# A linear-attention layer and a gated expert layer in one kernel: from units chunk by chunk to units batch by batch, with some whole-batch loads

## The chip, the cores and the metric

The kernel runs on one core of a Trainium2 chip. The metric is the device time of one execution in microseconds. Three runs before the change gave 155.5, 156.43 and 154.58 us, a median of 155.5. The profile is of one execution more, with a span of 152.4 us from the first to the last instruction that it shows.

## What is computed

There are 4 batches, 8 heads, 768 tokens and 48 numbers a head. The first half is a recurrent attention with a decay for each number, the second a layer with a softmax-like gate and a normalisation:

```python
for t in range(S):                       # state: [B, H, 48, 48]
    y[t] = r[t] @ (state + (u * k[t])^T v[t])
    state = w[t][:, None] * state + k[t]^T v[t]
x = y as [B * S, H * D]                  # 3072 x 384
h = x @ w_in                             # 3072 x 1024
solu = h * softmax(h)
ln = (solu - mean(solu)) / sqrt(var(solu) + 1e-6) * g_ln
out = ln @ w_out                         # 3072 x 384
```

All inputs and the output are fp32; the matrix products are made in bf16.

## The kernel before, in words

**Units.** The 768 tokens of a batch are cut into 6 chunks of 128. A unit is one chunk of one batch, with all 8 heads: 24 units. Before, unit i is chunk i // 4 of batch i % 4 (line 117, `units`), so that the four batches take turns and a batch's state goes from unit i to unit i + 4.

**Stages.** Each unit goes through some forty stages, each a small function. The string `ORDER` (lines 21 to 67) lists every stage of every unit as a word: name, unit, and after a point where it is done (`a` ScalarE, `d` VectorE, `p` GpSimd, or a number, the bank of PSUM). The loop at the end (line 550) calls the functions word by word. The class `InOrder` (line 72) makes each engine keep this order in its own queue; SyncE, which issues all DMAs, too. So an instruction that waits holds up everything that stands behind it on its engine. Nearly all instructions carry line 86, the helper's; go by the tiles.

The words that matter here:

- `LW`, `LK`, `LR`, `LV` (lines 246 to 256): load w, k, r, v of a unit, 192 KB each, 8 heads of 48 numbers (192 B) for 128 tokens. They go into rings of 7 tiles (`NIO`), whose heads lie 64 numbers apart. k and r share the tile `kr_in`.
- `LI`, `LO`: load w_in in 3 parts and w_out in 2, into tiles of their own (`win_f`, `wout_f`); `wi` casts w_in to bf16, `gw` multiplies w_out by the gain, `mn`, `mc` and `ce` take off the column means.
- `lw` log of w (ScalarE), `cum` cumulated logs (TensorE), `ex` their exponentials (ScalarE), `kp` k and r scaled with them (VectorE), `krk` and `krr` the transposes of both (TensorE), `kr` their copy from PSUM.
- `p`, `q`, `qh`, `dg`, `dv`: the bonus term with u, on GpSimd and VectorE (`qh` folds the product in half first); `vb` the cast of v.
- `M`, `m`, `sel`: the scores of the chunk, their copy and mask. `Y`, `y`: attention out, with the state of the chunk before; `Y` with `i` adds the bonus by a product with the identity, with `n` the copy `y` adds it. `S`, `et`, `st`: the new state.
- `X`, `xT`: y transposed. `H`: the product with w_in, 24 matmuls. `e` exp, `he` h times exp, `hq` its square, `ea` two halves of e added, so that the sum of e takes 4 matmuls and not 8. `Oa`, `Ob`: the product with w_out, four of eight parts each, with the sums for the norm in three more columns of the same bank.
- `sq`, `qm`, `lv` (lines 518 to 527): the norm's scale rs = exp(-0.5 ln(...)), two ScalarE operations around one of VectorE and then two on ScalarE. `o`: the output times rs. `out`: the store of 192 KB.
- `hot`: matmuls on zeros at the start. `LU`, `us`, `uc` and `LG`, `gs`, `gc` bring u and the gain in.

**Memory.** PSUM is cut by hand into 8 banks; `H`, `M` and `cum` take two each.

Of the kernel before, what the change touches and what calls it, by code (L numbers as in the profile page):

```python
# [8 lines left out]
F32 = mybir.dt.float32  # L9
# [11 lines left out]
ORDER = """  # L21
LW2 LU0 ik0 lw2 hot5.4 cum2.0 LW1 lw1 us0.7 ih0 LW3 lw3 cum3.2 LR2 uc0 ex2 LK2 p2 LV2 vb2.p kp2 hot4.4 krk2.6 krr2
LR1 LK1 cum1.4 LW0 ex1 kp1 kr2.d hot1.0 S2.7 lw0 et2 LV1 vb1.d LW4 st2 p1 q1 hot2.0 krk1.1 krr1 q2 qh2 dg2 LG0
kr1.a M2.4 ex3 hot1.0 M1.6 m1.d dv2 LR0 LK0 p0 q0 cum0.0 ex0 lw4 cum4.6 ex4 kp0 krk0.1 krr0 LR3 gs0.0 gc0 dg1
m2.d Y2.i0 kr0.d LK3 p3 LR4 LV0 vb0.a dg0 dv1 kp3 Y1.i5 hot3.1 krk3.4 krr3 LK4 kp4 M0.2 m0.d krk4.1 y1.a X1.5
krr4 y2.a X2.0 dv0 xT2.d hot1.6 Y0.n7 y0.d kr3.a M3.2 hot1.0 X0.6 S1.4 p4 q3 kr4.a xT1.a xT0.a LI2 LI1 wi1.a
M4.0 m4.a et1 LI0 S0.5 et0 wi0.d m3.d LO1 wi2.p H1.6 e1 gw5.a H2.0 e2 H0.2 LO0 gw2.a q4 qh4 dg4 qh3 dg3 gw4.p
gw7.p LV3 vb3.p dv3 sel4 LW6 e0 gw6.d st1 LV4 vb4.p he1 lw6 dv4 gw1.d LW5 gw0.d gw3.d mn0.4 mc0 ce5.p ce6.p
Y3.i7 ce4.p he2 st0 he0 cum6.0 y3.a ce7.p hot1.5 X3.6 lw5 xT3.a ce3.d LK6 LR6 p6 Y4.n5 LR5 LK5 ce2.d hq0.a ex6
LW7 cum5.2 H3.6 p5 y4.d ex5 ce1.d ce0.d Oa0.5 kp6 krk6.1 krr6 S4.0 hq1.d Oa1.4 kp5 krk5.3 krr5 X4.2 Ob1 e3 he3  # L30
LV5 q6 q5 kr5.d hq2.a et4 st4 M5.6 kr6.a M6.0 xT4.d lw7 cum7.2 hq3.a sq1 m6.a m5.d dg5 vb5.d qm1 dv5 Ob0 ex7 sq0
qm0 S3.7 qh6 LR7 LK7 p7 kp7 et3 lv1 st3 lv0 H4.0 Y5.n6 y5.d LR9 LK8 o1.d e4 krk7.3 krr7 Oa2.2 he4 X5.7 q7 kr7.d
LW9 lw9 o0.a LK9 p9 LW8 lw8 S5.6 et5 cum9.4 ex9 Ob2 sq2 LR8 p8 st5 dg6 kp9 qm2 LV6 xT5.a LV9 vb6.p dv6 sel6
cum8.0 ex8 kp8 hq4.a LV7 LV11 out1 LW10 dg7 vb7.p dv7 Oa3.3 vb9.a lv2 H5.6 e5 M7.4 m7.d he5 q8 krk9.1 LK10 krr9
kr9.a S9.0 et9 Ob3 sq3 st9 q9 qm3 o2.a out0 ea5.p Y6.i5 y6.a LV8 LR10 Y7.n4 y7.d LW11 LW12 krk8.1 M9.6 lw10 lv3
X6.2 xT6.a m9.d o3.a krr8 LV10 out3 out2 kr8.d qh9 dg9 dg8 hq5.d cum10.4 ex10 kp10 S6.0 vb11.d et6 X7.2 xT7.a
st6 p10 vb8.d dv8 dv9 H6.6 e6 he6 H7.2 lw11 e7 he7 M8.4 m8.a Oa5.1 Y9.n0 Ob5 sq5 y9.d cum11.6 ex11 krk10.5 krr10
qm5 kr10.d S7.4 et7 st7 Oa4.3 hq6.d lv5 lw12 o5.a X9.2 sel8 Y8.i0 vb10.p y8.a LK11 LR11 kp11 xT9.d q10 dg10 p11
M10.4 m10.a sel10 S10.1 et10 st10 dv10 S8.0 et8 S11.7 et11 X8.6 xT8.a LK12 LW13 cum12.4 q11 ex12 lw13 st11 st8
Ob4 sq4 qm4 LW14 LR12 kp12 p12 lw14 lv4 o4.a out5 LK13 LV12 LR13 Y10.n2 dg11 y10.d H8.6 e8 krk12.1 krk11.0 krr11  # L40
krr12 kr12.d he8 kr11.a q12 qh12 cum13.4 H9.2 vb12.p S12.1 ex13 p13 q13 ea7.p dg12 kp13 dv11 LW16 LR14 LK14 e9
he9 et12 st12 M12.6 m12.a Oa6.0 X10.5 xT10.a krk13.4 krr13 kr13.a M11.6 m11.d ea8.p dv12 sel12 p14 cum14.2 ex14
q14 out4 Ob6 sq6 hq8.d M13.4 m13.d LV13 hq7.a LW15 lw15 lw16 kp14 vb13.d H10.6 dg13 qm6 LW18 lw18 Y11.n1 y11.d
Oa8.5 LK16 LR15 LR16 LK15 e10 he10 hq9.a krk14.4 Y12.i3 krr14 lv6 qh14 kr14.d p15 ea10.p dv13 LR18 LV14 vb14.p
q15 qh15 LK18 p18 Ob8 sq8 qm8 y12.a S13.2 et13 st13 o6.a lv8 X11.1 xT11.d cum16.6 ex16 X12.3 hq10.d LW19 kp16
Oa9.4 cum15.0 xT12.a Ob9 ex15 kp15 sq9 o8.a dg14 dv14 qm9 M14.2 m14.a sel14 krk16.7 Oa7.6 krr16 kr16.d lv9 o9.d
cum18.0 ex18 kp18 Ob7 LV15 S14.5 et14 st14 krk15.3 krr15 kr15.d LK19 Y13.i2 lw19 cum19.0 krk18.7 p16 q16 vb15.a
S15.4 y13.a sq7 qm7 dg15 X13.5 xT13.d ex19 LR19 kp19 lv7 o7.a q18 krr18 kr18.d H11.2 et15 st15 krk19.5 krr19
kr19.d LW17 lw17 cum17.0 e11 he11 ex17 ea11.p out8 LK17 LR17 p17 kp17 H12.6 e12 he12 hq11.a p19 H13.4 e13 Oa10.3
Y14.n2 M16.0 m16.a dg16 q19 dv15 y14.d ea12.p ea13.p M15.6 m15.d he13 Ob10 sq10 X14.2 out9 Oa11.1 LW20 qm10 lw20  # L50
cum20.6 hq12.d krk17.0 krr17 out6 out7 LV16 vb16.a dv16 xT14.a S16.2 LR20 ex20 LK20 dg18 et16 st16 lv10 o10.a
H14.4 e14 kp20 Ob11 sq11 kr17.d LK23 qm11 lv11 o11.a Oa12.2 krk20.3 krr20 kr20.a he14 sel16 Y16.n7 y16.d Y15.n6
y15.d M19.4 m19.a M18.0 m18.d Ob12 X15.7 xT15.a q17 hq13.d LV19 LW21 LV17 X16.3 xT16.a ea14.p vb19.a M17.4 m17.d
sq12 LK22 out10 qm12 dg17 qh19 vb17.p sel19 p20 hq14.a LW22 LV20 q20 qh20 dv17 M20.0 LV21 m20.d out11 LK21 H15.6
e15 he15 lw22 ea15.p H16.4 LV18 vb18.p dv18 LR21 p21 lw21 Oa14.3 Y17.n1 LR22 LV23 q21 dg19 dv19 Ob14 LR23 p23
p22 e16 he16 lv12 Oa13.0 LW23 o12.a out12 sq14 qm14 hq15.d vb20.a lv14 dg20 dv20 y17.d cum21.6 ex21 Ob13 cum22.4
sq13 ex22 LV22 vb22.p ea16.p o14.d out14 Y18.n2 y18.d Oa15.1 X18.3 qm13 kp22 lv13 xT18.d X17.2 xT17.a kp21 Ob15
sq15 qm15 S18.5 et18 st18 Y19.n4 y19.d lv15 o15.a out15 o13.a krk22.2 S17.3 et17 lw23 H18.6 e18 ea18.p hq16.d
vb21.d st17 Y20.n5 y20.d X19.4 xT19.d krr22 kr22.a H17.0 he18 hq18.d cum23.4 ex23 kp23 Oa16.3 e17 ea17.p he17
krk21.2 krr21 kr21.a H19.6 e19 krk23.5 X20.4 krr23 q22 qh21 vb23.p out13 xT20.a kr23.a he19 Oa18.2 Ob16 sq16  # L60
M21.0 q23 ea19.p qh23 dg22 dv22 m21.a sel21 qm16 lv16 M22.6 hq19.a M23.4 Ob18 sq18 dg21 H20.0 o16.a out16 m22.d
m23.d Oa19.7 Y22.n6 qm18 lv18 hq17.d Ob19 S19.5 dg23 dv23 e20 Oa17.4 y22.d X22.3 he20 et19 st19 xT22.d dv21
Y21.n6 Ob17 y21.d sq19 o18.a sq17 qm17 lv17 Y23.n1 out18 qm19 lv19 X21.0 xT21.d H22.2 o17.a e22 out17 ea20.p
y23.d H21.0 X23.5 xT23.a e21 hq20.d o19.d out19 Oa20.6 he22 hq22.d H23.4 e23 he21 hq21.d Ob20 sq20 qm20 lv20
o20.a out20 ea22.p Oa22.7 ea21.p Oa21.3 he23 hq23.d Ob22 sq22 qm22 lv22 Ob21 sq21 qm21 lv21 o21.d o22.a out22
out21 ea23.p Oa23.2 Ob23 sq23 qm23 lv23 o23.a out23
"""

NIO, NLW, NKP, NWK = 7, 10, 6, 4
# [24 lines left out]
def kernel(  # L94
# [22 lines left out]
    units = [(c, b) for c in range(NC) for b in range(B)]  # L117
# [30 lines left out]
    w_t = ring("w_in", NIO, [C, H, 64], F32)  # L148
    kr_t = ring("kr_in", NIO, [C, 2, H, 64], F32)
    v_t = ring("v_in", NIO, [C, H, 64], F32)  # L150
    win_f = consts.tile([128, KM, DF], F32)
    wout_f = consts.tile([128, KF, DM], F32)
    o_t = ring("o", NWK, [C, DM], F32)
# [28 lines left out]
    dve.memset(inv_col, 1.0 / RDF)  # L182
    ones_row = consts.tile([1, C], F32)
# [23 lines left out]
    st_t = [ring(f"st{b}_", 2, [C, H, D], BF16) for b in range(B)]  # L207
    xT_t = ring("xT", NWK, [128, KM, C], BF16)
    e_t = ring("e", NWK, [128, KF, C], BF16)
    ea_t = ring("ea", NWK, [128, KF // 2, C], BF16)  # L210
    he_t = ring("he", NWK, [128, KF, C], BF16)
    hq_t = ring("hq", NWK, [128, KF, C], BF16)
    sq_t = ring("sq", NWK, [C, 2], F32)
    qm_t = ring("qm", NWK, [C, 1], F32)
    lv_t = ring("lv", NWK, [C, 1], F32)
# [26 lines left out]
    def rows_of(src, i):  # L242
        c, b = units[i]
        return src[b, :, c * C:(c + 1) * C, :].rearrange("h t d -> t h d")

    def load_w(i, x):
        sp.dma_start(out=w_t[i % NIO][:, :, :D], in_=rows_of(w, i))

    def load_k(i, x):
        sp.dma_start(out=kr_t[i % NIO][:, 0, :, :D], in_=rows_of(k, i))  # L250

    def load_r(i, x):
        sp.dma_start(out=kr_t[i % NIO][:, 1, :, :D], in_=rows_of(r, i))

    def load_v(i, x):
        sp.dma_start(out=v_t[i % NIO][:, :, :D], in_=rows_of(v, i))
# [63 lines left out]
    def log_w(i, x):  # L320
        act.activation(out=lw_t[i % NLW][:, :, :D], in_=w_t[i % NIO][:, :, :D], func=LN)
# [11 lines left out]
    def scaled(i, x):  # L333
        ex = live[i]["ex"][:, :, :DM].rearrange("t a (h d) -> t a h d", h=H)
        dve.tensor_mul(out=kp_t[i % NKP][:, :, :, :D], in0=ex, in1=kr_t[i % NIO][:, :, :, :D])

    def bonus_rk(i, x):
        kr = kr_t[i % NIO]
        pool.tensor_mul(out=p_t[i % 3], in0=kr[:, 0, :, :D], in1=kr[:, 1, :, :D])
# [10 lines left out]
    def v_cast(i, x):  # L350
        copy = {"a": act.copy, "d": dve.tensor_copy, "p": pool.tensor_copy}[x]
        copy(out=vb_t[i % NLW], in_=v_t[i % NIO][:, :, :D])
# [49 lines left out]

    def attend(i, x):
        L = live[i]
        c, b = units[i]
        m, kr, vb = m_t[i % NWK], kr_s[i % NKP], vb_t[i % NLW]
        y_ps = L["y_ps"] = bank([C, DM], F32, x[-1], "y_ps")
        first = True
# [175 lines left out]
```

## Time and profile before

| | |
|---|---|
| median of the runs | 155.5 us (154.58 to 156.43) |
| span of the profiled execution | 152.4 us |
| first wait for data, `lw` of unit 2 on ScalarE | starts at 3.43 us |
| `kp` on VectorE, 24 of 128x768 | mean 951 ns |
| `hq` on VectorE, 15; on ScalarE, 9 | mean 890 ns; 1055 ns |
| `p`, `q`, `ea` on GpSimd | mean 1038, 931, 1181 ns |
| `sq`, `lv`, `rs` on ScalarE, `qm` on VectorE, 24 each | mean 170, 294, 203, 151 ns |
| a load of 192 KB, issue to landing | median 3.6 to 3.7 us |
| w_in, 512 KB; w_out, 768 KB | median 6.4 us; 9.0 us |
| last load issued | 114.78 us |

Busy time is the time in which an engine has an instruction running; PE is TensorE, DVE VectorE, ACT ScalarE, POOL GpSimd, SP SyncE, and SPq its DMA issues. A stretch row gives from, to and length in us, then the busy us (and instructions) of the five engines, then the granted clock, the DMA engines' share and GB/s. A timeline row gives start and length in us.

### The profile page before, as it was taken

The page shows a single profiled execution, that of the slowest core. Times are in us where ns is not written, and L with a number is a line of the kernel's source. Part 1 is how long each engine was busy: PE and PEld are TensorE (multiplying, and loading weights), DVE is VectorE, ACT ScalarE, POOL GpSimd, SP SyncE. Part 2 cuts the span into 40 slices and gives each one's busy share as a digit, 9 for nine tenths or more (in the row PEclk, how much of TensorE's full clock was granted, in tenths as well). Part 3 has the DMA queues.
Part 4 walks back from the last instruction along what each step waited for, and adds up shares of the span by engine and source line. Part 5 has one row for each costly group of instructions (what it writes and reads, how often), then busy time and mean ns, then how long its engine had stood idle before and what let it go on. Part 6 is the DMA issues. An engine that isn't in the chain of part 4 may idle for free.

```text
span 152.4 us, 5172 instructions
## 1 busy us (share of the span) xinstructions
PE 136.4 (90%) x2093; PEld 105.5 (69%) x2093; DVE 131.8 (87%) x227; ACT 120.0 (79%) x247; POOL 119.0 (78%) x149
## 2 busy tenths in 40 slices
PE   6777598968999999999998999999799999999970
PEld 1242365936778889779776689887686988889740
DVE  5029968899999999998999999999999999988940
ACT  4526648869888999799998889998988789938661
POOL 7268986799909994899999997799889979973600
PEclk9959969999999999999999999999999999999998
DMA  3999999989979999989897989995998110112023
GB/s 76 218 216 211 217 334 377 254 175 223 216 151 216 220 204 229 206 177 224 194 203 144 228 195 275 199 199 136 241 205 210 63 45 4 44 63 103 4 79 127
DMA packets 104825, 27.06 MB, mean 178 GB/s; under 512 B 100314, under 2 KB 104419, under 8 KB 104803
## 3 DMA queue, kind: packets, MB, share of 16 engines
q1 hardware_dynamic: 104802, 26.75, 77.4%
q8 instruction: 16, 0.26, 0.7%
q14 instruction: 7, 0.05, 0.1%
HBM read 22.03 MB, written 4.72 MB: 176 GB/s over the span
## 4 chain that ended last, share of the span: by engine, by line
PE 53%; DVE 23%; SPq 8%; ACT 6%; issue 3%; DMA 2%; POOL 1%; DVEq 0%; POOLq 0%
PE ps L86 53%; SPq L86 7%; DVE he L86 6%; DVE m L86 4%; DVE kp L86 4%; DVE w L86 3%; DMA kr_in<-in_k_dram 2%; DVE kr L86 1%; DVE hq L86 1%; DVE y L86 1%; DVE st L86 1%; ACT ps L86 1%; ACT o L86 1%; DVE dg L86 1%; ACT win_sb L86 1%
## 5 line engine op out<-in xcount | busy, mean ns | idle before, releaser
L86 PE MATMUL ps<-w,he 128*128 128x385 bf16 x192 | 44.5, 325 | 1.0 <-DVE w L86 0.7
L86 PE MATMUL ps<-xT,win_sb 128*128 128x128 bf16 x576 | 35.5, 219 | 1.1 <-DVE qm L86 0.8
L86 PEld LDWEIGHTS <-win_sb 128*128 128x128 bf16 x576 | 32.8, 98 | 2.2 <-DVE m L86 0.9
L86 PE MATMUL ps<-one_col,hq 128*128 128x1 bf16 x192 | 31.5, 164 | 0.0
L86 DVE TENSOR_TENSOR he<-ps,e 128x1024 bf16<-128x1024 f32 x24 | 29.1, 1214 | 1.6 <-ACT e L86 1.6
L86 DVE TENSOR_TENSOR kp<-ps,kr_in 128x768 bf16<-128x768 f32 x24 | 22.8, 951 | 7.7 <-DMA kr_in<-in_k_dram 4.9
L86 POOL TENSOR_TENSOR p<-kr_in 128x384 bf16<-128x384 f32 x24 | 24.7, 1038 | 4.5 <-DMA kr_in<-in_k_dram 4.2
L86 POOL TENSOR_TENSOR dv<-vb,dg 128x384 bf16<-128x384 bf16 x24 | 21.7, 907 | 7.5 <-DVE qm L86 3.6
L86 ACT ACTIVATE e<-ps 128x1024 bf16<-128x1024 f32 x24 | 24.5, 1021 | 3.1 <-PE ps L86 2.0
L86 POOL TENSOR_TENSOR ea<-e 128x512 bf16<-128x512 bf16 x17 | 20.0, 1181 | 6.4 <-ACT e L86 5.7
L86 POOL TENSOR_TENSOR q<-p,u_bc 128x384 bf16<-128x384 bf16 x24 | 22.2, 931 | 2.4 <-DVE dg L86 1.7
L86 ACT ACTIVATE ps<-ps 128x768 f32<-128x768 f32 x24 | 19.1, 799 | 5.1 <-PE ps L86 4.3
L86 PEld LDWEIGHTS <-kp 128*128 128x128 bf16 x272 | 17.5, 100 | 6.0 <-DVE kp L86 3.2
L86 PEld LDWEIGHTS <-he 128*128 128x128 bf16 x192 | 18.4, 96 | 4.0
L86 PEld LDWEIGHTS <-hq 128*128 128x128 bf16 x192 | 15.4, 96 | 8.3
L86 DVE TENSOR_TENSOR m<-ps,keep 128x1024 bf16<-128x1024 f32 x15 | 18.2, 1216 | 1.2 <-PE ps L86 1.0
L86 PE MATMUL ps<-ident,kp 128*128 128x128 bf16 x192 | 16.5, 227 | 1.6 <-POOL p L86 1.1
L86 DVE TENSOR_TENSOR hq<-he 128x1024 bf16<-128x1024 bf16 x15 | 13.4, 890 | 0.1
L86 ACT COPY kr<-ps 128x1024 bf16<-128x1024 bf16 x11 | 11.1, 1012 | 2.4 <-PE ps L86 2.4
L86 ACT ACTIVATE lw<-w_in 128x384 bf16<-128x384 f32 x23 | 11.7, 523 | 1.3 <-DMA w_in<-in_w_dram 1.3
L86 PEld LDWEIGHTS <-kr 64*128 64x128 bf16 (+1 forms) x272 | 10.2, 95 | 3.1 <-ACT kr L86 0.7
L86 PE MATMUL ps<-inv_col,ea 128*128 128x1 bf16 x68 | 11.2, 165 | 0.0
(90 smaller groups left out, 293.7 us busy)
## 6 DMA issues: line engine op xcount, KB each, us to landing
w_in<-in_w_dram SPq DMA_DIRECT2D x24, 192.0 KB, 3.7
kr_in<-in_r_dram SPq DMA_DIRECT2D x24, 192.0 KB, 3.7
kr_in<-in_k_dram SPq DMA_DIRECT2D x24, 192.0 KB, 3.7
v_in<-in_v_dram SPq DMA_DIRECT2D x24, 192.0 KB, 3.6
out_dram<-o SPq DMA_DIRECT2D x24, 192.0 KB, 2.6
win_f<-in_moe_w_in_dram SPq DMA_DIRECT2D x3, 512.0 KB, 6.4
wout_f<-in_moe_w_out_dram SPq DMA_DIRECT2D x2, 768.0 KB, 9.0
u_row<-in_u_dram SPq DMA_DIRECT2D x1, 1.5 KB
```

The costliest lines, as they stand in the source:

```text
L86: made = make(*args, **kwargs)
```

## The change

Six things change together.

1. Unit i becomes chunk i % 6 of batch i // 6: all of batch 0, then batch 1, and so on. The state goes from unit i to unit i + 1, in a ring of 3 tiles in place of 2 for each batch.
2. The inputs lie in two tiles `in`, one for an even batch and one for an odd, each with k, r, w and v of a whole batch, heads and chunks packed with 48 numbers each. Batches 0 and 1 are loaded by unit as before; batches 2 and 3 by one transfer of 1152 KB for each tensor (words `BW`, `BK`, `BR`, `BV`). A large load waits until all that read the tensor of two batches before have done so.
3. w_out is staged in the last third of the second `in` tile, where w and v of batch 1 go later; w_in in a tile `late`, in which the outputs `o` lie afterwards.
4. The norm's scale: `sq` is two VectorE operations from PSUM; `rs` is a subtraction and a power of -0.5 on GpSimd. `qm` and `lv` are gone.
5. `ORDER` is another. By engine, before and after: `hq` 15 on VectorE and 9 on ScalarE, then 3 and 21; `ea` 17, then 20; `qh` 12, then 7; `Y` with the identity 7, then 5; `kr` 11 on ScalarE and 13 on VectorE, then 8 and 16; `o` 19 and 5, then 14 and 10; `hot` 19 matmuls, then 23.
6. Functions for further ways (`ht`, `kt`, `xt`, `sv`, `by_rows`) come in; no word of the new order uses them.

The order of SyncE's queue, from which the loads follow:

```
before: LW2 LU0 LW1 LW3 LR2 LK2 LV2 LR1 LK1 LW0 LV1 LW4 LG0 LR0 LK0 LR3 LK3 LR4 LV0 LK4 LI2 LI1 LI0 LO1 LO0 LV3
        LW6 LV4 LW5 LK6 LR6 LR5 LK5 LW7 LV5 LR7 LK7 LR9 LK8 LW9 LK9 LW8 LR8 LV6 LV9 LV7 LV11 out1 LW10 LK10 out0 ...
after:  LU0 LW0 LK0 LR0 LW1 LK1 LR1 LI0 LV0 LI1 LV1 LI2 LG0 LW2 LK2 LR2 LV2 LO0 LO1 LW3 LK3 LR3 LV3 LW4 LK4 LR4 LV4
        LW5 LK5 LR5 LV5 LW6 out0 LK6 LR6 out2 LV6 LW7 LK7 LR7 LV7 LW8 LK8 LR8 LV8 BW2 LW9 LK9 LR9 LV9 BK2 LW10 LK10
        LR10 LV10 BR2 out3 out4 out1 LW11 LK11 LR11 LV11 BV2 BW3 BK3 BR3 out5 out8 out7 out6 out9 BV3 out10 ...
```

And the new order where the first unit of batch 3 comes in:

```
... cum18.1 lw20 kr16.a ex18 Ob9 y13.d xT12.d dg15 cum20.6 dv14 xT11.d sq9 kp18 H10.3 krk18.5 sel14 cum19.1 ex20
rs9 p17 kp20 krr18 o9.a p19 q17 kr18.d e10 ex19 he10 Y14.n0 kp19 H12.6 ...
```

The diff, cut to its core:

```diff
-    units = [(c, b) for c in range(NC) for b in range(B)]
+    units = [(b, c) for b in range(B) for c in range(NC)]
...
-    w_t = ring("w_in", NIO, [C, H, 64], F32)
-    kr_t = ring("kr_in", NIO, [C, 2, H, 64], F32)
-    v_t = ring("v_in", NIO, [C, H, 64], F32)
-    win_f = consts.tile([128, KM, DF], F32)
-    wout_f = consts.tile([128, KF, DM], F32)
-    o_t = ring("o", NWK, [C, DM], F32)
+    in_t = ring("in", 2, [C, 4, H, NC, D], F32)
+    staged = in_t[1].rearrange("p s h c d -> p (s h c d)")
+    wout_f = staged[:, 4 * H * NC * D - KF * DM:].rearrange("p (a n) -> p a n", a=KF)
+    late = consts.tile([128, KM * DF], F32, name="late")
+    win_f = late.rearrange("p (a n) -> p a n", a=KM)
+    o_t = [late[:, j * DM:(j + 1) * DM] for j in range(NWK)]
...
-    st_t = [ring(f"st{b}_", 2, [C, H, D], BF16) for b in range(B)]
+    st_t = ring("st", 3, [C, H, D], BF16)
...
+    def load(src, kind, i):
+        b, c = units[i]
+        sp.dma_start(out=chunk(kind, i), in_=src[b, :, c * C:(c + 1) * C, :].rearrange("h t d -> t h d"))
+
+    def load_all(src, kind, b):
+        sp.dma_start(out=in_t[b % 2][:, kind], in_=src[b].rearrange("h (c t) d -> t h c d", t=C))
...
     def sums(i, x):
-        act.activation(out=sq_t[i % NWK], in_=live[i]["o_ps"][:, DM:DM + 2], func=SQUARE)
-
-    def variance(i, x):
-        dve.tensor_sub(out=qm_t[i % NWK], in0=live[i]["o_ps"][:, DM + 2:], in1=sq_t[i % NWK][:, 0:1])
+        o_ps = live[i]["o_ps"]
+        square = s2_t[i % NWK] if i in by_rows else o_ps[:, DM + 2:]
+        dve.tensor_scalar(out=var_t[i % NWK], in0=o_ps[:, DM:DM + 1], scalar1=o_ps[:, DM:DM + 1], scalar2=square,
+                          op0=MULT, op1=SUB)
+        if i not in by_rows:
+            total = o_ps[:, DM + 1:DM + 2]
+            dve.tensor_scalar(out=eps_t[i % NWK], in0=total, scalar1=total, scalar2=1e-6 * DF * DF, op0=MULT, op1=MULT)
...
     def scale(i, x):
-        act.activation(out=lv_t[i % NWK], in_=sq_t[i % NWK][:, 1:2], func=LN, scale=1e-6 * DF * DF,
-                       bias=qm_t[i % NWK])
-        act.activation(out=rs_t[i % NWK], in_=lv_t[i % NWK], func=EXP, scale=-0.5)
+        rs = rs_t[i % NWK]
+        pool.tensor_tensor(out=rs, in0=eps_t[i % NWK], in1=var_t[i % NWK], op=SUB)
+        pool.tensor_tensor(out=rs, in0=rs, in1=minus_half, op=ALU.pow)
```

## The prediction, made before the changed kernel was run

> **What bounds the kernel now.** I read the page first, then the table by stretches of time, then the chain of work that ended last, then the timelines of SyncE (its DMA queue) and TensorE. The page:
>
> ```profile
> span 152.4 us, 5172 instructions
> PE 136.4 (90%) x2093; PEld 105.5 (69%) x2093; DVE 131.8 (87%) x227; ACT 120.0 (79%) x247; POOL 119.0 (78%) x149
> ...
> DMA  3999999989979999989897989995998110112023
> GB/s 76 218 216 211 217 334 377 254 175 223 216 151 216 220 204 229 206 177 224 194 203 144 228 195 275 199 199 136 241 205 210 63 45 4 44 63 103 4 79 127
> DMA packets 104825, 27.06 MB, mean 178 GB/s; under 512 B 100314, under 2 KB 104419, under 8 KB 104803
> ```
>
> Two resources run without a break. TensorE is busy for 90%. The DMA engines are full from the second slice to the thirtieth (115 us), at some 200 GB/s, and nearly all their packets are under 512 B: a load of one tensor for one unit is 1024 rows of 192 B. In the slices at 335 to 377 GB/s the weights come, whose rows are 1.5 and 4 KB long. The stretches show it more sharply (last two columns: DMA share, GB/s):
>
> ```profile
> 3.00:8.00 5.00, 3.54 (x12) 1.05 (x10) 0.33 (x3) 2.64 (x5) 1.70 (x9) 1.00 1.01 200
> 8.00:13.00 5.00, 3.86 (x33) 2.41 (x34) 2.40 (x4) 1.32 (x4) 3.65 (x5) 0.66 1.04 206
> 22.00:25.00 3.00, 2.71 (x45) 1.82 (x44) 2.05 (x3) 2.40 (x3) 2.83 (x5) 1.00 1.01 378
> 60.00:65.00 5.00, 5.00 (x84) 3.79 (x82) 5.00 (x10) 4.20 (x10) 3.62 (x5) 1.00 1.02 204
> ```
>
> So at full DMA share a 192 KB load (196,608 B) takes 0.96 us at 204 GB/s, 0.98 at 200, 0.92 at 214 (the stretch from 5 to 10 us). The chain of work:
>
> ```profile
> 13.35 3.79 DMA kr_in<-in_k_dram
> ...
> 43.27 31.86 PE ps L86 x551
> ...
> 110.34 37.23 PE ps L86 x601
> 147.57 0.02 issue
> 147.60 0.18 ACT sq L86
> ```
>
> The chain runs through SyncE's issues and a load up to 17 us, through weights and VectorE up to 43, and then TensorE carries it to 147.57. In the list of waits nothing after 43 us waits for a DMA: the loads stay just ahead, because the queue takes them in the order in which the units need them. The last output takes 4.8 us from TensorE's end to the span's end.
>
> TensorE's prices are distances from start to start in its timeline: 24 matmuls of H 1.50 us; half an output 0.81 with summed e (139.62 to 140.43), 0.86 without; both cumulations 0.33; four transposes 0.23 (39.08 to 39.53 for eight); M 0.40; S 0.46; Y 0.41; X 0.18. With them, what stands in its queue from 43.94 us on adds up to 106.1 us; it took 103.6. I scale by 0.976.
>
> **The change part by part.**
>
> TensorE: three more units with summed e save 3 x 0.1 us, two fewer Y with an identity product 2 x 0.17. About -0.6 us. Four more warm-up matmuls lie in the idle start; if they delay the first units, 4 x 0.4.
>
> ScalarE: squares and scales gone, -4.1 -7.1 -4.9; twelve more hq, +12.7; the moved copies (kr, m, vb, xT, y, o, gains) sum to -4. Net -7.5 us of 120. VectorE: twelve hq fewer, -10.7; sub gone, -3.6; two small operations per unit, 48 x 0.15 = +7.4; the rest +3. Net -4 of 132. Both lie beside TensorE and are worth little by themselves.
>
> GpSimd: three more ea +3.5, a sel +1.2, a weight cast +1.0, five half-additions fewer -2.7, a gain fewer -1.2, and per unit a subtraction and a power on 128x1. No row shows a power there. Below is 0.1 us each (its 128x1 memsets); above, 0.93 each (a 128x384 product). I take 0.35 a pair, nearer the memsets because the element count is theirs; +8 us in all, ends +5 and +45. Behind rs wait p, q and ea on GpSimd, and o on the engine that reads the bank.
>
> Tail: sq, qm, lv, rs (0.92 us from 147.60 to 148.52) become two VectorE operations (0.3) and the GpSimd pair (0.2 to 1.9). Taken as 0, ends -0.4 and +1.3.
>
> Loads: bytes and rows stay the same, 96 x 1024 rows of 192 B, in 48 loads by unit and 8 of six times the size. A large load cannot have longer rows in DRAM, as a head's 48 numbers of one token are all that is contiguous there. Its destination is contiguous now, but so was that of w_out before (6 KB a partition), and its packets stayed at 1.5 KB: 104,419 - 100,314 = 4,105 is 24 x 128 rows of the stores plus 1024 rows of w_out. So I price a large load at 6 x 0.96 = 5.8 us. Ends: 3.2 us, if its 1.18 MB ran at the weights' 369 GB/s (20 to 25 us), and 7 us, should rows cost more whose destination no longer starts at multiples of 256 B (the old rings had 64 numbers a head, the new tile has 48). The source rows start at multiples of 192 B already and ran at 200 GB/s, so I stay at 5.8.
>
> The Trainium skill, DMA: Bandwidth & Descriptors, section Rules for kernel authors, asks for at least 1 MiB per DMA, and its section Bandwidth measures 341 GB/s at 1 MB; by that a large load is an estimated 3.5 us. That speaks for the change and is the first rival below; the same page's Specifications put line rate at 512 B and up, as the trace has it (200 GB/s on short rows, 378 on long).
>
> The order of the loads is the step that decides. SyncE's queue up to the r of batch 3 (word BR3) now holds: 48 loads by unit (units 0 to 11), seven large ones (w, k, r, v of batch 2; w, k, r of batch 3) worth 42, together 90 x 0.96 = 86.4 us; w_in 3 x 1.42 and w_out 2 x 2.13 (at 369 GB/s) = 8.5; five stores at the same rate 2.7. First data: the first load was issued at 0.79 and used at 3.43, so 1.7 us after issue; the new one goes second, issued at 1.28: 2.9. Landing lag 0.4 (the eighth load was used at 10.51). A store of unit 0 now stands ahead of k of unit 6, and SyncE waits there for o0. I followed unit 0 from row to row: w_out lands at 23.5 instead of 27 to 29.5, gains and mean to 27, four GpSimd centrings of 0.83 to 30.6, output to 32.8, sq behind he1 and rs behind p3, o0 done at 35. By then the queue is drained (35.6), and data flows again 1.7 us after the issue: 2 us lost; ends 0 and 5. Sum: 2.9 + 86.4 + 8.5 + 2.7 + 0.4 + 2 = 103 us. Ends: 99 (0.92 a load, no gap) and 109 (0.98, gap 5, and 97% share, the mean from 20 to 110 us).
>
> Who waits for it: kp18 on VectorE (needs k and r of batch 3), and behind it on VectorE kr18, kp20, kp19, he10; on TensorE krk18, and behind it all the rest; on ScalarE e10. GpSimd waits at p19. Nothing covers it: by 36.5 us TensorE has some 16.5 us of its work done on the same hand-followed path, so without this wait it would stand at krk18 (68.0 us of its prices) near 87. Before that it is held the same way more gently: w of unit 10 (position 37.5) lands near 64, v of batch 2 (position 54) near 85. The eighth large load, v of batch 3, stands behind out9 and so behind kp18; it lands near 115, and S18, its first user on TensorE, comes 26 us of work after krk18: no wait.
>
> What is left for TensorE from krk18 on: 13 H 19.5, 28 half outputs 22.7, 12 transposes of four 2.8, 4 cumulations 1.3, 9 M 3.6, 10 Y 3.9, 7 S 3.1, 11 X 2.0 = 58.9, scaled 57.5. VectorE's rest by its row means is 56.6, GpSimd's 53, ScalarE's 49, all beside it. The restart costs something: the granted clock was 0.66 from 8 to 13 us, after idle time. I take 1 us, ends 0 and 3.4.
>
> Sum: 103 + 1.0 (kp18) + 57.5 + 1 + 4.8 = 167.4 span. The runs' median 155.5 stands 3.1 above the profiled span 152.4. Forecast 170.5. Low end 99 + 1 + 57.5 + 4.4 + 3.1 = 165; high end 109 + 1 + 57.5 + 3.4 + 6.1 + 3.1 = 180.
>
> **The rivals.**
>
> (a) Large loads go at the rate of long rows, so they cost 3.2 us. For it: the two largest transfers of the trace (512 and 768 KB) are also the fastest. Against: these had long rows, and w_out's packets did not grow. BR3 lands at 103 - 7 x 2.6 = 85 and no longer holds; w of unit 10 (lands near 61) does: 61.5 + 89.4 x 0.976 + 4.8 + 3.1 = 157, or 152 without any such wait (36.5 + 110.4 x 0.976 + 7.9). I say 155. This is what the Trainium skill's rule above would have. Not slower from a price of 3.8 us a large load down (170.5 - 7 x 2.0 = 156.5).
>
> (b) Rows of 192 B write more slowly where they start at multiples of 192 B. At +12% (7% to 25%): 90 x 0.12 = 11 us, 181 to 192. For it: no row shows such a destination. Against: the source side, as said.
>
> (c) The power is slow and GpSimd becomes the bound after the wait. It decides from about 0.8 us a pair on (its rest, 53 at row means, is some 50.5 in time, as neighbours overlap; 57.5 - 50.5 = 7 us over 15 pairs, added to 0.35); at 1.5 us a pair its rest is some 68 us and the time 180. For it: its two-operand rows are its slowest. Against: 128 numbers, one a partition.
>
> That the change does nothing is excluded: the order of the loads becomes another.
>
> **How the numbers follow.** Forecast 0.70 (165 to 180), (a) 0.10, (b) 0.10, (c) 0.10. The range 161 to 183 leaves out (a) and the upper parts of (b) and (c), under 2 in 10. The likeliest case's own range is 165 to 180. A measurement of this kernel can tell 1% from no change. Of (a), 0.04 is faster by over 1% (under 154), 0.06 within; the rest, 0.90, is slower.
>
> **What would show it.** In the changed kernel's profile: DMA share full until some 110 us at 200 to 215 GB/s, also while the large loads run (wrong if these show 300 GB/s or more); kp on VectorE waits for a DMA of k or r near 100 us and the chain of waits has it; TensorE idles some 15 us between 45 and 105 and is dense after; p and ea no slower than now. It is wrong if TensorE is dense from 45 us on, or if GpSimd is over 95% after 105.

## The result and the profile after

The changed kernel takes 176.05 us (median of 4 runs, 175.87 to 178.13), the kernel before 155.04 us in the same runs: a ratio of 1.137, 95% interval 1.129 to 1.146. It is slower, by 21 us where 15 were forecast. The profiled execution took 175.89 us with a span of 174.2.

The page of the changed kernel, the lines that answer to those of before:

```profile
span 174.2 us, 5109 instructions
PE 144.4 (83%) x2082; PEld 108.0 (62%) x2083; DVE 129.8 (75%) x243; ACT 114.7 (66%) x181; POOL 134.7 (77%) x196
...
PE   7967778956989854999989856999898989989990
...
PEclk9999999999999996599999998799999999999998
DMA  4999999799899889999899695831201011020012
GB/s 91 205 337 255 307 233 201 153 232 215 169 235 186 183 186 208 234 239 217 181 228 215 136 235 201 208 68 45 96 36 37 27 45 49 0 78 34 31 75 106
DMA packets 67321, 27.07 MB, mean 155 GB/s; under 512 B 50521, under 2 KB 66914, under 8 KB 67298
```

TensorE has fallen from 90% to 83% of a longer span, with dips around 39, 65 and 105 us. The DMA engines work until the 26th slice, which ends at 113 us, with gaps near 98 and 107. In the last line, 50,521 packets are under 512 B where 100,314 were. The table by stretches shows the two later dips (from, to, length, then busy us of TensorE, its weight loads, VectorE, ScalarE and GpSimd, then clock, DMA share, GB/s):

```profile
60.00:65.00 5.00, 3.37 (x59) 2.64 (x57) 3.58 (x7) 2.02 (x3) 4.37 (x9) 1.00 0.87 207
65.00:70.00 5.00, 2.36 (x24) 1.37 (x24) 1.79 (x3) 2.23 (x5) 1.93 (x3) 0.67 0.94 197
70.00:75.00 5.00, 5.00 (x61) 4.07 (x58) 3.04 (x7) 3.27 (x7) 2.84 (x4) 0.64 1.07 258
100.00:105.00 5.00, 2.61 (x37) 2.03 (x35) 1.54 (x6) 1.59 (x2) 3.88 (x6) 1.00 1.08 251
105.00:110.00 5.00, 3.77 (x47) 3.52 (x48) 4.44 (x5) 2.19 (x3) 3.47 (x4) 0.77 0.48 163
125.00:130.00 5.00, 4.64 (x74) 3.61 (x70) 4.33 (x10) 4.61 (x6) 4.69 (x8) 1.00 0.10 37
```

From 65 to 70 and from 100 to 105 TensorE is busy for about half of the time, VectorE and ScalarE for less, while the DMA share is 0.94 and 1.08. What ends the second dip stands in the timelines of VectorE and ScalarE (start, length, engine, line, operation; in brackets the idle time before and what ended it):

```profile
105.11 1.82 DVE L82 TENSOR_TENSOR kp<-ps,in 128x768 bf16<-128x768 f32 x2 [3.58 <-DMA in<-in_r_dram]
...
106.55 0.58 ACT L82 ACTIVATE late<-ps,rs 128x384 f32<-128x384 f32 x1 [4.39 <-DMA out_dram<-late]
```

The first row is kp18 with kp20 behind it: it starts at 105.11, when the r of batch 3 has landed; 103 was forecast. The second row is o9, and it was not foreseen. The outputs lie in a ring of 4 tiles, so o9 needs the tile of o5, whose store stands in SyncE's queue behind that same large load. krk18 starts at 106.13. TensorE ends at 169.4, 63.3 us later; `var` of the last output starts right behind it:

```profile
169.48 0.29 DVE L82 TENSOR_SCALAR var<-ps 128x1 f32<-128x1 f32 x1 [0.39 <-PE ps L82]
```

The lines of the new scale (ns min/median/max):

```profile
L82 POOL TENSOR_TENSOR rs<-eps,var x24: 187/191/569, 33.6 to 170.0; 128x1 f32<-128x1 f32 x24
L82 POOL TENSOR_TENSOR rs<-rs,minus_half x24: 550/551/568, 33.9 to 170.2; 128x1 f32<-128x1 f32 x24
```

A subtraction and a power take 0.74 us, and 0.81 with the gap of 0.07 between them. I had taken 0.35.

### The profile page after: what moved, and what is told of

Same layout as the page of the kernel before. It is cut to its first block, busy times and chain, and to the rows that moved or that the text cites. A ratio compares the mean times of both kernels' runs of the same rounds, so it can differ in the third digit from the quotient of the medians.

```text
span 174.2 us, 5109 instructions
## 1 busy us (share of the span) xinstructions
PE 144.4 (83%) x2082; PEld 108.0 (62%) x2083; DVE 129.8 (75%) x243; ACT 114.7 (66%) x181; POOL 134.7 (77%) x196
## 2 busy tenths in 40 slices
DMA packets 67321, 27.07 MB, mean 155 GB/s; under 512 B 50521, under 2 KB 66914, under 8 KB 67298
## 3 DMA queue, kind: packets, MB, share of 16 engines
q1 hardware_dynamic: 67298, 26.75, 64.4%
## 4 chain that ended last, share of the span: by engine, by line
SPq 25%; POOL 24%; PE 15%; DMA 14%; DVE 13%; issue 4%; ACT 3%; POOLq 0%; ACTq 0%; DVEq 0%
SPq L82 24%; PE ps L82 15%; POOL rs L82 7%; DMA out_dram<-late 5%; DMA in<-in_r_dram 5%; DMA in<-in_moe_w_out_dram 4%; POOL p L82 4%; POOL q L82 4%; POOL dv L82 3%; DVE he L82 3%; POOL ea L82 3%; POOL m L82 3%; DVE m L82 2%; ACT late L82 2%; DVE kp L82 2%
## 5 line engine op out<-in xcount | busy, mean ns | idle before, releaser
L82 PE MATMUL ps<-xT,win_sb 128*128 128x128 bf16 x576 | 37.0, 223 | 0.8 <-DVE xT L82 0.4
L82 PEld LDWEIGHTS <-win_sb 128*128 128x128 bf16 x576 | 34.2, 100 | 2.8 <-issue 1.3
L82 POOL TENSOR_TENSOR p<-in 128x384 bf16<-128x384 f32 x24 | 24.0, 1006 | 9.2 <-DMA in<-in_r_dram 9.2
L82 DVE TENSOR_TENSOR kp<-ps,in 128x768 bf16<-128x768 f32 x24 | 22.6, 951 | 8.7 <-ACT ps L82 4.3
L82 POOL TENSOR_TENSOR ea<-e 128x512 bf16<-128x512 bf16 x20 | 23.1, 1155 | 6.8 <-ACT e L82 5.6
L82 ACT ACTIVATE e<-ps 128x1024 bf16<-128x1024 f32 x24 | 24.3, 1021 | 5.5 <-PE ps L82 5.5
L82 ACT ACTIVATE hq<-he 128x1024 bf16<-128x1024 bf16 x21 | 22.1, 1058 | 1.6 <-DVE he L82 1.6
L82 POOL TENSOR_TENSOR dv<-vb,dg 128x384 bf16<-128x384 bf16 x24 | 20.3, 850 | 3.5 <-DVE dg L82 3.4
L82 ACT ACTIVATE late<-ps,rs 128x384 f32<-128x384 f32 x14 | 8.1, 581 | 15.7 <-POOL rs L82 8.4
L82 ACT ACTIVATE lw<-in 128x384 bf16<-128x384 f32 x23 | 11.9, 523 | 8.5 <-DMA in<-in_w_dram 8.5
L82 DVE TENSOR_TENSOR st<-ps,et 128x384 bf16<-128x384 f32 x20 | 11.0, 552 | 7.3 <-ACT et L82 7.3
```

Of the source, the lines that this page charges most:

```text
L82: made = make(*args, **kwargs)
```

## The experiments

Three theories came up. *Queue*: what stands late in SyncE's queue sets the end, and the rest behind it is fixed. *GpSimd* (in the first runs *scale*): the power makes GpSimd the bound. *Chain*: the order by batches, in which each unit's state comes from the unit ahead of it, cannot run denser. Kernels e1 to e4, e6 and e8 each do or undo one thing; e7 is a kernel of loads and stores alone; the others build on these.

| kernel | us | ratio to before (95%) | kp18 starts | TensorE ends | between |
|---|---|---|---|---|---|
| changed | 176.05 | 1.137 (1.129 to 1.146) | 105.11 | 169.48 | 64.4 |
| e1 loads by unit, by need | 176.69 | 1.146 (1.138 to 1.153) | 106.20 | 169.50 | 63.3 |
| e2 r of batch 3 by unit | 176.52 | 1.146 (1.138 to 1.153) | 103.04 | 170.25 | 67.2 |
| e3 unit loads first | 178.33 | 1.158 (1.150 to 1.165) | 109.34 | 172.65 | 63.3 |
| e4 old scale | 175.56 | 1.139 (1.129 to 1.149) | 104.94 | | |
| e5 = e1 + ring of 8 outputs | 166.38 | 1.074 (1.065 to 1.082) | 96.78 | 160.35 | 63.6 |
| e6 large loads left out | 166.51 | 1.077 (1.070 to 1.084) | 96.42 | 159.71 | 63.3 |
| e8 before + power | 186.87 | 1.209 (1.199 to 1.220) | | | |
| e9 = e6 + old scale | 167.89 | 1.082 (1.079 to 1.085) | 98.08 | | |
| e10 = e6, state two units back | 166.84 | 1.075 (1.072 to 1.078) | 96.68 | 160.65 | 64.0 |
| e11 = e5 + old scale | 168.63 | 1.088 (1.084 to 1.093) | 97.31 | | |
| e12 = e11 + engines as before | 184.24 | 1.188 (1.179 to 1.197) | | | |

TensorE's end is read where `var` of the last output starts, which is not there with the old scale. The expectations of e4 and e6 take 62.5 us from krk18 to TensorE's end and 5.5 us behind it; that was counted to the last output but one. To the last output it is 63.3 us, and 4.8 behind it.

**e1, loads by unit in the order of need**

```diff
- LV8 BW2 LW9 LK9 LR9 LV9 BK2 ... LW10 LK10 ... BR2 ... BV2 BW3 BK3 ... BR3 ... BV3
+ LV8 LW12 LW9 LK9 LR9 LV9 LW14 LW13 LW10 LV10 LK10 LR10 LW16 LW15 ... LK13 LR13 ...
```

> The eight large loads and the unit loads from unit 9 on become 60 loads by unit, in the order of their first use; everything else stays as changed. Three theories. Queue: the r of batch 3 lands late (105.0 us) because it stands behind the work of 90 loads, and what follows it is fixed; here the k and r of unit 18 stand behind some 75 loads and should land near 90, so krk18 starts near 91 to 93 and not at 106, and the time is 155 to 163 us. Scale: GpSimd, with the subtraction and the power at some 0.75 us a unit, is what sets the end; it has the same work here, so the time stays above 170. Chain: units of one batch hang together through the state, one after the other, and TensorE could not be denser whatever the loads do; the time stays near 176.

Measured: 176.69 us, no gain, where the queue theory had 155 to 163. It failed in this form, and the timeline of ScalarE says why:

```profile
87.21 0.58 ACT L83 ACTIVATE late<-ps,rs 128x384 f32<-128x384 f32 x1 [11.04 <-DMA out_dram<-late]
```

The loads were no longer late, but o5 waited 11.04 us for the store of unit 1, which SyncE issued at 83.70 behind the loads that I had moved ahead of it; kp18 came at 106.20, as late as in the changed kernel. The edit had exchanged a late load for a late store. So it told nothing apart; e5 does.

**e2, only the r of batch 3 by unit**

```diff
- BR3
+ LR18 LR19 LR20 LR21 LR22 LR23
```

> Only the large load of r of batch 3 becomes six loads by unit, in the same place of the queue. Queue: the r of unit 18 lands one unit load after the k of batch 3 and not six, so 5 x 0.96 = 4.8 us earlier, near 100; the waits of kp18 shrink by as much, the time is near 171 (169 to 173); less if the store of unit 5, which still stands behind all six, then holds o9. Scale and chain: no change beyond 1 us, 175 to 177.

Measured: 176.52 us. From the timelines of VectorE and of ScalarE:

```profile
103.04 1.81 DVE L81 TENSOR_TENSOR kp<-ps,in 128x768 bf16<-128x768 f32 x2
...
107.42 0.58 ACT L81 ACTIVATE late<-ps,rs 128x384 f32<-128x384 f32 x1 [3.68 <-DMA out_dram<-late]
```

kp18 starts 2.1 us sooner and has no wait for a DMA in its brackets. o9 still waits for the store of unit 5, behind the same six loads, and starts 0.9 us later than before the edit. That is the exception named in the expectation. The large load and the store behind it are two holds that end at the same place of the queue; taking one away gives nothing.

**e3, units 9 to 11 ahead of the large loads**

```diff
- LV8 BW2 LW9 LK9 LR9 LV9 BK2 ... LW10 LK10 ... LR10 LV10 ... BR2 ... LW11 LK11 ... LR11 ... LV11
+ LV8 LW9 LK9 LR9 LV9 LW10 LK10 LR10 LV10 LW11 LK11 LR11 LV11 BW2 BK2 ... BR2
```

> The unit loads of units 9, 10 and 11 move ahead of the large loads of batch 2 in SyncE's queue; the sum of what stands ahead of the r of batch 3 is the same. Queue: the waits between 55 and 75 us go (w of unit 10 lands some 10 us sooner), k and r of batch 2 come some 10 us later, but the r of batch 3 lands at 105 as before, and the time stays at 176, give or take 2. If instead the early waits are what costs, the time falls by the 3 to 8 us that TensorE idled there.

Measured: 178.33 us, 0.3 above the range of the queue theory; no gain. ScalarE now waits for the w of batch 2 instead:

```profile
67.44 0.52 ACT L81 ACTIVATE lw<-in 128x384 bf16<-128x384 f32 x1 [12.44 <-DMA in<-in_w_dram]
```

The word order has lw12 ahead of lw9, lw10 and lw11, so a large load is needed earlier than the three units that this edit put ahead of it. The stall of 12.4 us takes the place of the later ones: kp18 comes at 109.34 with no wait in its brackets, and 63.3 us later TensorE is done.

**e4, the old scale in the changed kernel**

```diff
- pool.tensor_tensor(out=rs, in0=eps, in1=var, op=SUB)
- pool.tensor_tensor(out=rs, in0=rs, in1=minus_half, op=ALU.pow)
+ act.activation(out=lv, in_=sq[:, 1:2], func=LN, scale=1e-6 * DF * DF, bias=qm)
+ act.activation(out=rs, in_=lv, func=EXP, scale=-0.5)
```

> The norm's scale goes back to ScalarE (square, a subtraction on VectorE, log, exp), everything else stays as changed. Queue: TensorE's rest after krk18 is 62.5 us where 58.5 was forecast, and the scale can be at most these 4 us of it; 172 to 176. Scale: GpSimd is freed of 24 x 0.75 = 18 us, some 11 of them after 105 us, and the time falls by 8 us or more, to 168 or below.

Measured: 175.56 us. GpSimd's busy time fell from 134.7 to 117.1 us and the time did not move. While the queue holds all engines, the power is not what costs.

**e5, e1 with a ring of 8 outputs**

```diff
- o_t = [late[:, j * DM:(j + 1) * DM] for j in range(NWK)]
+ o_t = [late[:, j * DM:(j + 1) * DM] for j in range(8)]
```

> The loads by unit in the order of need, as in the kernel e1, and a ring of 8 output tiles in place of 4, so that o of unit i waits for the store of unit i - 8 and no longer of unit i - 4, whose store stands behind loads in SyncE's queue. Queue (the queue of SyncE sets the end, through whatever stands late in it, a load or a store): the wait of 11.0 us for a store in e1 and the one of 2.6 go, and 155 to 166 us come out. Chain (the new order itself, with the state going from each unit to the next and the norm's scale over VectorE and GpSimd, cannot run denser): near 176, as in e1.

Measured: 166.38 us, 0.4 above the range of the queue theory and far from that of the chain theory; a ratio of 1.074 (1.065 to 1.082) where the changed kernel has 1.137. No output waits for a store now (o5 does not wait, o9 for 0.86 us, which the trace puts down to a load). Loads in the order of need and stores that hold nobody together give back 9 to 10 us. The loads alone give none (e1). The larger ring alone, with the large loads kept, was not run; kp18 would still have to wait there for the r of batch 3.

**e6, without the large loads**

```diff
- BW2 BK2 BR2 BV2 BW3 BK3 BR3 BV3
```

> The eight large loads are left out: units 12 to 23 compute on the inputs of batches 0 and 1 again. All other instructions stay in their order. So 9.4 of 27 MB are not moved, and no unit from 12 on can wait for a load. Queue: TensorE goes through from 36.5 us on with 110.4 us of its prices; at 0.976 the span is 149 and the time 151; with the rate seen after 106 us in the changed kernel (62.5 us for 58.9 of prices, a factor of 1.06) it is 36.5 + 117 + 5.5 = 159 and the time 161. Chain: 170 or more, as the waits for loads only took the place of other waits.

Measured: 166.51 us, between the ranges of the two theories (up to 161, and from 170). e5, which loads everything, is as fast as a kernel that does not load a third of the bytes. So the hold of the queue is worth some 9.5 us and not more, and 11 us stay that no large load causes. They have a place. The stretches of e6, then those of the kernel before:

```profile
50.00:75.00 25.00, 21.91 (x343) 17.10 (x343) 23.75 (x39) 20.38 (x35) 23.68 (x32) 1.00 0.57 123
75.00:100.00 25.00, 23.41 (x383) 18.52 (x382) 22.49 (x44) 22.18 (x36) 24.61 (x35) 1.00 0.11 41
```

```profile
50.00:75.00 25.00, 25.00 (x441) 20.82 (x438) 24.18 (x42) 23.33 (x52) 21.59 (x27) 1.00 0.96 210
75.00:100.00 25.00, 24.23 (x395) 19.55 (x391) 24.48 (x39) 22.83 (x48) 23.09 (x25) 1.00 0.96 203
```

From 100 to 150 both do the same number of matmuls, 773 and 774, and from 75 to 100 e6 does 12 fewer. From 50 to 75 it does 343 where the kernel before does 441. By 50 us it has done 32 fewer, and it falls back from 36 us on: 170 matmuls against 213 from 36 to 50. So most of the 11 us are lost between 36 and 75 us. GpSimd is busy for 23.68 of 25 us from 50 to 75 (VectorE for 23.75), and the chain of work that ended last runs mostly through it there; but from 75 to 100, where it is fuller still (24.61), little is lost. From 38.5 to 47.7 us that chain runs through SyncE's queue, where the loads of units 6 to 8 stand behind the stores of units 0 and 2, and ends in this wait for w:

```profile
47.74 0.52 ACT L81 ACTIVATE lw<-in 128x384 bf16<-128x384 f32 x1 [1.43 <-DMA in<-in_w_dram]
```

**e7, the price of a load**

```diff
- for word in ORDER.split(): ...
+ 24 loads into wide[:, j, c, :, :D]    # 64 numbers a head
+ 24 loads into packed[:, j, :, c, :]   # 48 numbers a head
+ 4 loads into whole[:, j]              # a whole batch
```

> The whole computation is left out and the stores write zeros; there are 24 loads of one unit's tensor into tiles with 64 numbers a head, then 24 into tiles with 48 packed numbers a head, then 4 whole-batch loads, each group after the one before has landed. My price of 0.96 us for 192 KB: 23 us for each group, and 5.8 us a whole-batch load. Long-row price: the third group takes 13 us. Packed rows dear: the second and third group take 25 to 29 us.

The timeline of VectorE, whose copies mark the landing of each group:

```profile
31.41 0.18 DVE L52 COPY seen<-wide 128x24 f32<-128x24 f32 x1 [30.16 <-DMA wide<-in_v_dram]
...
56.18 0.18 DVE L58 COPY seen<-packed 128x24 f32<-128x24 f32 x1 [24.36 <-DMA packed<-in_v_dram]
...
81.47 0.18 DVE L62 COPY seen<-whole 128x24 f32<-128x24 f32 x1 [24.88 <-DMA whole<-in_v_dram]
```

From the first issue (0.72, 31.85 and 56.67 us) the groups take 30.7, 24.3 and 24.8 us. The stretches of the three groups and of the stores (from, to, length, two engines, clock, DMA share, GB/s):

```profile
3.00:31.00 28.00, 0.00 (x0) 0.00 (x0) 1.00 1.48 161
34.00:56.00 22.00, 0.00 (x0) 0.00 (x0) 1.00 1.04 205
60.00:80.00 20.00, 0.00 (x0) 0.00 (x0) 1.00 0.99 214
82.00:95.00 13.00, 0.00 (x0) 0.00 (x0) 1.00 0.98 345
```

Less the 1.7 us from an issue to its first data (the prediction's figure, from the kernel before), a packed unit load is 0.94 us and a whole-batch load 5.8: the price that I had taken. Packed rows are not dearer; the wide ones were, in this kernel (below).

**e8, the kernel before with the power alone**

```diff
- act.activation(out=sq, in_=o_ps[:, DM:DM + 2], func=SQUARE)
- dve.tensor_sub(out=qm, in0=o_ps[:, DM + 2:], in1=sq[:, 0:1])
- act.activation(out=lv, ..., func=LN, ...); act.activation(out=rs, in_=lv, func=EXP, scale=-0.5)
+ dve.tensor_scalar(out=var, ...); dve.tensor_scalar(out=eps, ...)
+ pool.tensor_tensor(out=rs, in0=eps, in1=var, op=SUB); pool.tensor_tensor(..., op=ALU.pow)
```

> The kernel before with nothing changed but the norm's scale, which goes from ScalarE to two VectorE operations and a subtraction and a power on GpSimd. 24 x 0.75 us come to GpSimd's 119 us of 152. If the scale costs only what it adds where GpSimd has room: 154 to 158. If GpSimd's order is what sets the end as soon as the pair is in it: over 160.

Measured: 186.87 us, 32 us slower than the kernel before, for 24 x 0.81 = 19 us of GpSimd's work. Its timeline from 129.8 us on, and under it one row of ScalarE's:

```profile
129.82 0.99 POOL L86 TENSOR_TENSOR p<-kr_in 128x384 bf16<-128x384 f32 x1
130.89 0.91 POOL L86 TENSOR_TENSOR q<-p,u_bc 128x384 bf16<-128x384 bf16 x1
131.75 0.83 POOL L86 TENSOR_TENSOR dv<-vb,dg 128x384 bf16<-128x384 bf16 x1
132.54 1.95 POOL L86 TENSOR_TENSOR p<-kr_in 128x384 bf16<-128x384 f32 x2
134.45 0.19 POOL L86 TENSOR_TENSOR rs<-eps,var 128x1 f32<-128x1 f32 x1
134.71 0.56 POOL L86 TENSOR_TENSOR rs<-rs,minus_half 128x1 f32<-128x1 f32 x1
...
135.31 0.58 ACT L86 ACTIVATE o<-ps,rs 128x384 f32<-128x384 f32 x1 [8.73 <-POOL rs L86]
```

ScalarE stands for 8.73 us before an output, waiting for an rs of 0.75 us that is queued on GpSimd behind p, q and dv of later units. In the list of waits this is 44.7 us in 14 waits on ScalarE alone. The word `rs` kept the place that it had for ScalarE, and GpSimd reached that place only after the work of other units. So it is the place in the queue that costs here. In the changed kernel, whose order is another, the same waits on ScalarE come to 8.4 us.

**e9, e6 with the old scale** (edits of e6 and e4)

> The kernel e6 (the eight large loads left out, units 12 to 23 compute on the inputs of batches 0 and 1) with the norm's scale back on ScalarE and VectorE. GpSimd theory: in e6 GpSimd is busy for 4.8 to 5.0 of 5 us from 50 to 95, and TensorE waits behind it; freed of 24 x 0.75 = 18 us, some 10 of them there, the time falls from 166.5 to 154 to 159. Chain theory (units of one batch hang together through the state, whatever GpSimd does): it stays at 164 to 167. If ScalarE, which gets 12 us more, takes GpSimd's place: 162 to 167 as well, with ScalarE near full in the windows where GpSimd is now.

Measured: 167.89 us. The GpSimd theory, 154 to 159, falls in this form. Nearest is the third way on record (162 to 167), with ScalarE near full:

```profile
75.00:100.00 25.00, 21.81 (x351) 17.13 (x349) 20.42 (x37) 23.08 (x49) 22.05 (x26) 1.00 0.09 33
```

From 75 to 100 ScalarE is busy for 23.08 of 25 us, GpSimd no longer full, and TensorE for 21.81 (23.41 in e6). The new order gives 21 of 24 hq to ScalarE, and here the scale comes on top of them. That ScalarE is what holds the others is argued from its busy time; e12 tries it.

**e10, e6 with the state of two units before**

```diff
- st = st_t[(i - 1) % 3]
+ st = st_t[(i - 2) % 3]
```

> The kernel e6 (large loads left out) with the state of two units before read in place of that of the unit before, so that no unit's S and Y wait for the state that the unit ahead of it makes; this leaves out one link of the recurrence. Chain theory: the time falls from 166.5 by 5 us or more, to 155 to 161. GpSimd theory: 165 to 167, as GpSimd's work is the same.

Measured: 166.84 us, kp18 at 96.68 and 64.0 us from there: as e6 (96.42 and 63.3). The link from state to state costs nothing here, with GpSimd as busy as in e6, and the chain theory falls in the form in which I had put it.

**e11, e5 with the old scale** (edits of e5 and e4)

> All inputs loaded, by unit in the order of need, a ring of 8 outputs (as e5) and the norm's scale back on ScalarE and VectorE: everything of the change that was suspected undone, the order by batches left. GpSimd theory: 154 to 159, level with the kernel before or up to 2% slower. Chain theory: 164 to 167, as e5.

Measured: 168.63 us, with all loads what e9 is without the large ones. That is above the ranges of both theories, 1.6 us above that of the chain theory.

**e12, e11 with the engines of before**

```diff
- hq0.a hq1.a hq2.a hq3.a ...   # 21 on ScalarE, 3 on VectorE
+ ...                           # 9 and 15, and kr, vb, xT, o too, as in the order before
```

> The kernel e11 (loads by unit in the order of need, ring of 8 outputs, the scale on ScalarE) with hq, the copies kr, vb and xT, and the output o of each unit on the engine that the kernel before gave them: 15 hq on VectorE and not 3, so some 10 us from ScalarE to VectorE. The order of the words stays. Split theory (ScalarE, with 125.7 us and full from 70 to 90, is now what the others wait for, as GpSimd was in e5): the time falls from 168.6 to 156 to 162. Order theory (the order by batches, planned with other engines in mind, makes the engines wait for each other whichever of them has the work): 165 or more.

Measured: 184.24 us, where the split theory had 156 to 162 and the order theory 165 or more; 16 us slower than e11, though beside TensorE no engine has more than 134 us of work (VectorE 133.7, ScalarE 121.2, GpSimd 120.2). From 50 to 100:

```profile
50.00:100.00 50.00, 41.87 (x644) 33.02 (x642) 40.51 (x63) 35.65 (x72) 37.53 (x43) 0.96 0.97 194
```

Nothing is full: 41.87, 40.51, 35.65 and 37.53 of 50 us on TensorE, VectorE, ScalarE and GpSimd, with the DMA engines near full as in the kernel before. The engines wait for each other in turn: in this stretch the list of waits has GpSimd waiting for ScalarE and VectorE, ScalarE for TensorE, TensorE for VectorE, and none for a load. As in e8, work that changes its engine and keeps its place among the words is dear in a fixed order.

## Why the prediction was right, and where its sizes were off

Its main step held: the r of batch 3 behind the work of 90 loads holds kp18, and TensorE idles around 65 and 105 us. But this hold is some 9.5 of the 21 us. The other 11 stay without it, and the prediction's sum had no term for them. e6, which has no such hold at all, takes 166.5 us and lies in the forecast's range too, so the time by itself does not show the mechanism; the rows at 105 us do. That the sum came near is in part luck (4). TensorE idles for 10 us from 45 to 105, where some 15 were forecast, and from 110 on it is busy for 55.9 of 59.4 us (41.7 of 42.5 from 105 on in the kernel before): dense, but less so than forecast. By the prediction's own terms:

1. **SyncE's queue: 103 forecast, 105.1 measured** (range 99 to 109). With the terms that it names, the ends come to 97 and 110, and the measured time lies inside either way. The w of unit 10 was used at 67.07, after a wait of 3.9 us, where about 64 was forecast.
2. **A large load at 5.8 us: 5.8 in e7.** The reason beside it was wrong. I had said that its packets cannot grow. They did: the page counts 66,914 - 50,521 = 16,393 packets from 512 B to 2 KB, 4,105 before, so 12,288 more, and 8 x 6,144 rows are four times 12,288. On average four rows of 192 B went into a packet of 768 B, at no gain in rate. Rival (a) falls: a large load ran at 214 GB/s in e7 and at 181 to 228 in the changed kernel's slices from 78 to 96 us, the stores with their rows of 1.5 KB at 345. The Trainium skill, DMA: Bandwidth & Descriptors, asks for 1 MiB a DMA in its section Rules for kernel authors and puts the line rate at 512 B and up in its Specifications. These loads had 1.18 MB and packets of 768 B and were no faster than loads by unit, so the measurement differs, if the size of a packet is what the page means. In these runs the rate goes with the rows: at most 214 GB/s in e7 with rows of 192 B, 378 in the kernel before with the 1.5 and 4 KB of the weights.
3. **The rest from krk18: 57.5 + 1 forecast, 63.3 measured.** The largest miss of the sum, +4.8. The wait of o9 is at most 1.1 of it: from kp18 on the changed kernel needs 64.4 us and e6, which has no such wait, 63.3. The factor of 0.976 was that of the kernel before, and the new order does not reach it: counted from the forecast's 36.5 us, e6 takes 159.7 - 36.5 = 123.2 us for my 110.4 us of prices, a factor of 1.12 with no large load in the way.
4. **The floor without the wait: krk18 near 87 forecast; in e6 kp18 starts at 96.4, and krk18 about 1 us behind it.** So the hold was worth 9 us and not 16, and the other 11 us of the loss are slower progress elsewhere. My sum came out near because the hold and the slow progress do not add: until 105 the one covers the other. That is luck, as the slow progress was not in the sum.
5. **Tail 4.8 forecast, 4.8 measured; time over span 3.1 and 1.7.** The 3.1 set the median of three runs against the span of a fourth; run by run it is 1.7 in the kernel before, too (154.12 with a span of 152.4). The whole: +2.1 (krk18), +4.8, -1.4 on 170.5 gives 176.0; the profiled run took 175.9, and the forecast's terms add up to 167.3 and not 167.4.
6. **Not in the sum at all:** the ring of 4 outputs and stores in the loads' queue. In the changed kernel this ends 1.4 us behind the r of batch 3 and so costs little; in e1 it held o5 for 11.

Of the rivals, (b) falls by e7. (c) needed 0.8 us a pair; the pair takes 0.81. GpSimd is indeed nearly full from 50 to 100 in e5 and e6, but not where I had put it: from 125 to 150 it is busy for 22.7 of 25 us in the changed kernel, and neither e4 nor e9, which take the pair away, is faster by more than half a us.

**What stays open.** The 11 us between e5 and the kernel before lie mostly from 36 to 75 us. Four causes were tried by themselves: the large loads (e6), the scale (e9, e11), the link of the state (e10), the split of the work over the engines (e12). None accounts for them alone. The scale and the link were not undone together, and the stores of units 0 and 2, behind which the loads of units 6 to 8 stand in all of these kernels, were not moved; the chain of e6 runs through them from 38.5 to 47.7 us. e8 and e12 show that an edit which moves work to another engine needs a new order of all words to be fair, and no such order was made here. So it is not settled whether an order by batches must be slower or this one is. No version was faster than the kernel before; e5 came nearest.

## What to carry to other kernels

In a queue that works in order, count everything ahead of what is waited for, stores as well as loads, and ask of each store which ring tile waits for it. A hold can be priced from its rows, but what its removal would give needs the floor under it: a kernel with the transfers left out shows that in one run, and e5 reached that floor. In a written-out order, an operation is worth its place as much as its duration: a scale of 0.81 us, put on another engine at its old place, cost 32 us over 24 units.

## What the runs showed of the hardware beyond that

- A power on 128x1 takes 0.55 us on GpSimd, a subtraction of the same size 0.19, a memset 0.10.
- In e1 TensorE did nothing from 80 to 85 us; the granted clock was 0.64 in that stretch, 0.50 in the next 5 us and 0.83 in the 5 after. Behind this stall the 24 matmuls of an H took 2.45 us (from 89.71 us on), where 1.50 is usual. In the changed kernel the clock was 0.67 and 0.64 from 65 to 75. So a stall costs a little more than its length.
- The wide unit loads of e7 ran at a steady 161 GB/s, the same rows into packed tiles at 205 GB/s. In the kernel before, loads into tiles of the same pitch ran at 200 and more, so the pitch alone does not explain it; the cause was not looked for.
